# Two attention blocks on one core: the build order as a written list, some projections as column tiles, and eps sums on GpSimd

## The chip, the core and the metric

The kernel runs on one core of one Trainium2 chip. The metric is device microseconds per execution, from start to end of the program on that core. A run of the kernel is timed several times, and the median is given; a profile of one execution gives the span (first to last instruction) and what each engine did.

The engines: TensorE (PE in the profile, its weight loads PEld), VectorE (DVE), ScalarE (ACT), GpSimd (POOL), and SyncE (SP), which issues most DMAs.

## The reference

Two attention blocks over 2048 tokens, 640 features and 32 heads of 20 columns; their outputs are concatenated.

```
# block A, four segments of 512 tokens, s = 0..3, causal inside a segment
logits = q_s k_s^T * 20**-0.5 + mask
a_dot  = softmax(logits) v_s
a_mem  = (phi(q_s) M) / (phi(q_s) z + 1e-6)      # phi(t) = t+1 if t > 0 else exp(t)
o      = sigmoid(beta) * a_mem + (1 - sigmoid(beta)) * a_dot
M += phi(k_s)^T v_s;  z += sum(phi(k_s))
out_A = concat(o) wo_A
# block B, causal with a sliding window of 256 tokens
out_B = softmax(masked q k^T * 20**-0.5) v wo_B
```

Everything is bfloat16 outside, with float32 sums on the chip.

## The kernel before

The work is cut into eight chunks of 512 tokens, taken in turn: A0, B0, A1, B1, A2, B2, A3, B3. For each chunk PE makes q and k (`qk_job`, five pieces each, five matmuls of 512 columns a piece), v (`v_job`, two halves of four token tiles, five matmuls of 320 columns each), the scores (`score_batch`, L758), the products of weights and v (`av`, L827; `av_tile`, L848, in the last chunk), for A1 to A3 the product with the memory (`mem`), and the output projection (`final_job`, `last_job`). Projection and memory matmuls go through one helper, `wide` (L870), which issues a single 128x128 matmul.

Three shapes of matmul tile follow each other on PE: scores use four row groups of 20 rows (four heads at once; some batches, on the edge squares of the masks, have key tiles of 64 columns: 64 small matmuls in a batch); `av` uses four column tiles of 32 columns at tile positions (0, 32j), again four heads at once; `wide` and `dm_job`, which updates the memory, use the whole array.

PSUM holds three double banks for scores (`sc`) and two single banks (`m`, made by `bank()`) for everything else. A group of `wide` matmuls or an `av` fills one of the two; it is free again when VectorE has copied it (L501, L677, L682, L1027) or transposed it into `tt` (`turn`, L883).

ScalarE turns each score bank into exps (`pt`, L774). GpSimd cuts the masks out of them (`affine_select`, L813), VectorE does the masks of the edge batches by a product with `ends` (L791). After an `av` or a `mem`, `norm` works on the transposed tile: a reciprocal of the sums (L908), and on GpSimd the product with it (L918). For a `mem` the sums first get eps added on VectorE (L903), then the reciprocal (L906), the product goes to `u`, and VectorE adds `u` to `o` (L931).

The order of all this is set when the program is built. `Flow` keeps a clock for each engine with prices for each kind of work (`on_pe`, `on_dve`, `on_pool`, `on_act`, `on_dma`). The loop in `body` asks at each step what can run at the PE clock: first the next batch of scores (unless `may_wait()` says that ScalarE has enough), then the first of `pend` (`av` and `mem` in the order in which they came up, a `mem` right behind its `av`), then the first job of `jobs + fins` (projections as generators that yield what they wait for). `room()` holds score batches and `av` back when more than 160 PE matmuls were issued in the last 3000 ns of this clock. Work for VectorE, GpSimd and the DMA queue is issued by `at`, `when_idle` and `blocked` as the clocks pass. On the chip each engine then runs its instructions in that order and waits on semaphores.

## Time and profile before

| what | value |
|---|---|
| the three timed runs | 336.43, 333.79, 334.89 us, median 334.89 |
| the profiled execution | 334.4 us, its span 331.6 us |
| PE matmuls busy | 315.6 us, 6583 instructions (6619 weight loads, 174.4 us) |
| ScalarE | 302.4 us, 333 instructions |
| VectorE | 264.2 us, 556 instructions |
| GpSimd | 256.3 us, 648 instructions |
| exps (L774) | 306, 1012 ns mean |
| masks on GpSimd (L813) | 512, 374 ns mean |
| transposes (L883) | 88, 711 ns mean |
| eps sums on VectorE (L903) | 24, 371 ns mean |
| granted PE clock | 1.000 |

The table is of the profiled execution but for its first row. Busy times of one engine can overlap: a matmul's time runs until its result is out, and the next one starts earlier, so what one matmul costs is read from the distance of starts. The chain of work that ended last goes back from the last instruction to what released it, step by step. In a row of waits the numbers are the total in us, how many times, and the longest. In a timeline row they are the start, the time until the end of the last merged instruction, the engine, the line, and how many were merged.

### The profile page before, as it was taken

The numbers are of one execution on the slowest core, as the hardware profiler recorded it, in microseconds if no ns is written. First come the engines' busy times: TensorE is split into PE (matmuls) and PEld (weight loads), VectorE is DVE, ScalarE is ACT, GpSimd is POOL, SyncE is SP. The second block draws the span as 40 slices with busy tenths as digits, with TensorE's granted clock in tenths as the row PEclk, the third lists the DMA queues.
The fourth block names the chain that finished last, engine by engine and source line by source line (L and its number), as shares of the span: only waits on it lengthen the run. The fifth ranks groups of instructions, "written<-read, shape, count | busy, mean of one in ns | idle before, by whom it ended". The sixth has DMA issues, their size and how long they took to land.

```text
span 331.6 us, 15794 instructions
## 1 busy us (share of the span) xinstructions
PE 315.6 (95%) x6583; PEld 174.4 (53%) x6619; DVE 264.2 (80%) x556; ACT 302.4 (91%) x333; POOL 256.3 (77%) x648
## 2 busy tenths in 40 slices
PE   8999999999999999989999999999999999999896
PEld 3444546455444455546644545455654545666564
DVE  6777767798978899989868898888667889876654
ACT  1979999999999999999999999989999999999841
POOL 8366689998659799975867879996875969977750
DMA  6975746566596852335699145044555154769852
GB/s 198 396 253 152 173 135 125 136 175 176 132 226 132 165 155 63 67 86 122 183 208 181 42 94 156 3 104 80 148 140 114 21 150 122 166 142 187 178 127 100
DMA packets 76260, 47.36 MB, mean 143 GB/s; under 512 B 48381, under 2 KB 73181, under 8 KB 76189
## 3 DMA queue, kind: packets, MB, share of 16 engines
q1 hardware_dynamic: 75469, 45.71, 56.7%
q8 instruction: 51, 0.84, 1.1%
q10 hardware_dynamic: 720, 0.66, 0.7%
q14 instruction: 20, 0.16, 0.2%
HBM read 17.62 MB, written 16.96 MB: 104 GB/s over the span
## 4 chain that ended last, share of the span: by engine, by line
PE 57%; DVE 15%; ACT 10%; issue 7%; POOL 6%; DMA 3%; SPq 1%; ACTq 0%; DVEq 0%; POOLq 0%
PE m L870 36%; PE sc L758 11%; ACT pt L774 10%; PE m L827 6%; POOL pt L813 4%; DVE pt L791 4%; PE m L848 2%; DVE tt L883 2%; POOL u L918 2%; DVE pq L542 2%; DVE kA L501 2%; DVE vA L677 1%; DMA xT<-in_A_x_dram 1%; DVE pq L536 1%; DVE ot L1027 1%
## 5 line engine op out<-in xcount | busy, mean ns | idle before, releaser
L774 ACT ACTIVATE pt<-sc 128x1024 bf16<-128x1024 f32 (+2 forms) x306 | 285.0, 1012 | 10.7 <-PE sc L758 8.6
L813 POOL TENSOR_SCALAR_AFFINE_SELECT pt<-pt 128x128 bf16<-128x128 bf16 (+1 forms) x512 | 177.1, 374 | 60.4 <-ACT pt L774 57.4
L883 DVE STREAM_TRANSPOSE tt<-m 128x512 f32<-128x512 f32 x88 | 61.4, 711 | 20.0 <-PE m L827 9.1
L918 POOL TENSOR_TENSOR o<-tt,rr 128x320 bf16<-128x320 f32 x64 | 47.8, 747 | 4.1 <-DVE rr L908 4.0
L870 PEld LDWEIGHTS <-xT 128*128 128x128 bf16 x350 | 32.0, 97 | 24.2 <-issue 12.3
L758 PE MATMUL sc<-qB,kB 20*64 20x64 bf16 (+2 forms) x1728 | 38.6, 218 | 1.4 <-issue 0.8
L791 DVE TENSOR_TENSOR pt<-pt,ends 128x1024 bf16<-128x1024 bf16 (+2 forms) x50 | 36.3, 740 | 0.0
L758 PEld LDWEIGHTS <-kB 20*64 20x64 bf16 (+1 forms) x1728 | 21.7, 98 | 23.3 <-issue 22.0
L758 PE MATMUL sc<-qA,kA 20*64 20x64 bf16 (+4 forms) x1024 | 33.1, 237 | 0.5
L1027 DVE CAST ot<-m 128x320 bf16<-128x320 f32 x56 | 26.9, 485 | 7.4 <-PE m L870 7.1
L870 PEld LDWEIGHTS <-oT 128*128 128x128 bf16 x280 | 24.7, 98 | 11.4 <-issue 1.1
L870 PE MATMUL m<-wBv,xT 128*128 128x320 bf16 x160 | 27.0, 299 | 2.4 <-DVE tt L883 2.3
L870 PE MATMUL m<-wv_A,xT 128*128 128x320 bf16 x160 | 26.0, 299 | 2.0 <-DVE vA L677 1.9
L870 PE MATMUL m<-xT,wBq 128*128 128x512 bf16 x96 | 26.4, 381 | 0.4 <-issue 0.2
L870 PE MATMUL m<-xT,wq_A 128*128 128x512 bf16 x88 | 25.0, 381 | 1.8 <-DVE vA L677 0.8
L870 PE MATMUL m<-xT,wk_A 128*128 128x512 bf16 x96 | 25.6, 388 | 1.1 <-DVE qA L501 0.7
L870 PE MATMUL m<-xT,wBk 128*128 128x512 bf16 x84 | 24.8, 381 | 0.8
L758 PEld LDWEIGHTS <-kA 20*128 20x128 bf16 (+1 forms) x1024 | 13.5, 97 | 20.6 <-issue 19.6
L827 PE MATMUL m<-pt,vA 128*32 128x192 bf16 (+3 forms) x512 | 23.6, 275 | 0.0
L870 PE MATMUL m<-wo_A,oT 128*128 128x320 bf16 x140 | 22.7, 300 | 0.2
L501 DVE CAST kB<-m 128x512 bf16<-128x512 f32 x20 | 13.8, 691 | 9.4 <-PE m L870 9.4
L870 PE MATMUL m<-wo_B,oT 128*128 128x320 bf16 x120 | 19.4, 300 | 0.3 <-DVE ot L1027 0.3
(112 smaller groups left out, 405.3 us busy)
## 6 DMA issues: line engine op xcount, KB each, us to landing
out_dram<-ot SPq DMA_DIRECT2D x29, 160.0 KB
scr_o<-o SPq DMA_DIRECT2D x28, 160.0 KB
xT<-in_B_x_dram SPq DMA_DIRECT2D x8, 288.0 KB
xT<-in_A_x_dram SPq DMA_DIRECT2D x8, 256.0 KB
scr_pk<-e SPq DMA_DIRECT2D x15, 128.0 KB
vS<-vA SPq DMA_DIRECT2D x16, 87.0 KB
vL<-vB SPq DMA_DIRECT2D x8, 174.0 KB
scr_kA<-kA SPq DMA_DIRECT2D x16, 60.0 KB
```

What stands on the lines that cost most here:

```text
L501: nc.vector.tensor_copy(out=dst[:, m, at:at + L], in_=ps[:, :])
L542: nc.vector.tensor_tensor(out=r if len(box) == 1 else e, in0=r, in1=e, op=ALU.min)
L758: nc.tensor.matmul(ps[j // 2][h0:h1, j % 2, c0:c0 + nq], lhsT=k[rows, g, k0:k0 + h1 - h0], rhs=q[rows, g, q0:q0 + nq], start=True, stop=Tr ...
L774: nc.scalar.activation(out=pt[:, :, lo:hi], in_=ps[i][:, :, lo:hi], func=ACT.Exp, scale=self.scale)
L791: nc.vector.tensor_tensor(out=blk, in0=blk, in1=self.ends[:, c0, :].unsqueeze(1).unsqueeze(1) .to_broadcast([P, 2, n // SH, SH]), op=ALU.mult)
L813: nc.gpsimd.affine_select(out=blk, in_=blk, pattern=pat, compare_op=ALU.is_ge, fill=self.zero, base=base, channel_multiplier=mul)
L827: nc.tensor.matmul(O[HD * j:HD * j + HD, q0:q0 + nq], lhsT=v[:, at_head(h):at_head(h) + HD], rhs=pts[j // 2][:, j % 2, c0:c0 + nq], start= ...
L848: nc.tensor.matmul(O[HD * j:HD * j + HD, o0:o0 + nq], lhsT=v[:, at_head(h):at_head(h) + HD], rhs=pts[j // 2][:, j % 2, c0:c0 + nq], start= ...
L870: self.nc.tensor.matmul(ps[:, 0:n], lhsT=lhsT, rhs=rhs, start=start, stop=stop)
L883: self.nc.vector.transpose(out=tt[:], in_=O[:, :])
L918: nc.gpsimd.tensor_tensor(out=to[:] if add_to else to, in0=a, in1=b, op=ALU.mult)
L1027: nc.vector.tensor_copy(out=ot[:, 320 * hf:320 * hf + 320], in_=ps[:, 0:320])
```

## The change

A list, `PLAN`, now says what the builder's loop does next. Its marks: `S` or `s` is a batch of scores, `A` an `av` (or `av_tile`), `M` a `mem`; `q20*5` is five steps of the job that makes q of chunk 2 from piece 0 on, and k, v, o, d (the memory's update) and z (the last block) likewise. The loop takes only the item that the list wants and moves its PE clock on until the item can run; the old conditions hold only where the list has ended. `M` has a queue of its own (`memq`) and is no longer bound to come right behind its `A`; it needs the `norm` of that `A` to have been issued.

A capital `S` says more: if an `A` follows before the next batch of scores, all `wide` matmuls in between (projections and `mem`) are issued as four column tiles of 32 columns, the shape of the `A`.

The sum with eps for a `mem` is made by GpSimd (`s0`), ahead of the reciprocal on VectorE (`s1`). The other edits are to the builder's clock: a limit of one block of 256 PE instructions per 3900 ns in place of `room()`, new prices for some VectorE work, and a model of GpSimd and VectorE holding each other up (`held`).

```
+PLAN = (
+    "k00*5 q00*5 k01*4 S k01 q01*5 S v00*16 S v00*4 k02 S k02*4 k03*5 q02*3 S q02*2 q03*5 k04*5 "
+    "A S A q04*5 v01 s v01*9 s k10*5 S v01*10 S q10*2 A S q10*3 q11*3 S q11*2 q12*5 A s k11*5 "
...
+    "q14*2 A q14 S d2*5 v11*4 S v11*8 S v11*3 A v11 S v11*4 d2*2 S q20*4 A s q20*5 s q20*6 "
...
+    "k30*6 S k30*4 q30 S q30*4 A s M q30*5 v30*2 s v30*3 A S M v30*10 s A M s v30*5 q33*4 S q33 "
...
+    "S q40*2 d4*2 A s M k40*5 s q40*10 S v40*5 k40*5 A S k40*5 v40*5 S v40*2 A v40*2 S v40*6 "
...
+    "o60*5 o70*5 S o70*2 A S o70*3 o71*5 o60*4 S o60*10 s o60 A o60*5 o71*5 o60*3 A o60*7 o72*2 "
+    "z0*4 ")
...
     def on_pe(self, mode, ns, cols, ready=0.0, n=1):
-        self.issued.append((max(self.pe, ready), n))
-        return self.on_pe_(mode, ns, cols, ready)
+        self.count += 1
...
+        self.on_pe_(mode, ns, cols, ready)
+        first, self.sent = self.sent, self.sent + 2 * n
+        at = (first - BLOCK0) // BLOCK + 1
+        while BLOCK * at + BLOCK0 <= self.sent:
...
+            wait = self.block - x
+            if wait > 0.0:
...
+                self.pe += wait
...
+            self.block = x + BLOCK_NS
+            at += 1
+        return self.pe + 215.0
...
     def wide(self, ps, lhsT, rhs, n, start, stop):
 
-        self.nc.tensor.matmul(ps[:, 0:n], lhsT=lhsT, rhs=rhs, start=start, stop=stop)
-        self.f.on_pe("full", mm_ns(n), n)
+        f = self.f
+        if self.by_tiles:
+            for j in range(4):
+                s = slice(HD * j, HD * j + HD)
+                self.nc.tensor.matmul(ps[s, 0:n], lhsT=lhsT[:, s], rhs=rhs, start=start,
+                                      stop=stop, tile_position=(0, HD * j),
+                                      skip_group_check=True)
+            f.on_pe("col", n / 2.4 + COL_NS, n, 0.0, 4)
+        else:
+            self.nc.tensor.matmul(ps[:, 0:n], lhsT=lhsT, rhs=rhs, start=start, stop=stop,
+                                  skip_group_check=True)
+            f.on_pe("full", mm_ns(n), n)
...
-        def s1():
+        def s0():
+            nc.gpsimd.tensor_single_scalar(out=rr[:], in_=tv[:, :, DH], scalar=EPS, op=ALU.add)
+            t = f.on_pool(EPS_NS, t0)
+            f.when_idle(t, lambda: s1(t))
+
+        def s1(te=None):
             if add_to:
-                nc.vector.tensor_single_scalar(out=rr[:], in_=tv[:, :, DH], scalar=EPS,
-                                               op=ALU.add)
-                f.on_dve(100.0, t0)
                 nc.vector.reciprocal(out=rr[:], in_=rr[:])
+                t1 = f.on_dve(276.0, te)
...
-        f.when_idle(t0, s1)
+        if add_to:
+            f.at(t0 - 100.0, s0)
+        else:
+            f.when_idle(t0, s1)
...
+        plan = PLAN.split()
+        plan = [x.split("*")[0] for x in plan for _ in range(int((x + "*1").split("*")[1]))]
+        visits, tiles = [False], False
+        for x in plan:
+            if x in "Ss":
+                visits.append(False)
+                tiles = x == "S"
+            elif x == "A" and tiles:
+                visits[-1] = True
...
+            want = plan[-1] if plan else None
+            self.by_tiles = bool(plan) and visits[i]
+            if i < len(bs) and want in (None, "S", "s"):
...
-                        if t <= f.pe and not self.may_wait():
+                        if t <= f.pe and (want or not self.may_wait()):
+                            if want:
+                                plan.pop()
...
-                                    pend.append((n, g, "mem"))
+                                    memq.append((n, g))
...
-            if pend:
+            if pend and want in (None, "A"):
...
+            if memq and want in (None, "M"):
+                n, g = memq[0]
...
+                if want and jb[2] != want and (jb[2][0] != "d" or jb[1] in ("bank", 0.0)):
+                    continue
```

## The prediction, made before the changed kernel ran

> **What bounds the kernel now.** I read the page's busy row first, then the chain of work that ended last, the timeline of short stretches, the waits of PE, and the DMA queues.

> ```profile
> span 331.6 us, 15794 instructions
> PE 315.6 (95%) x6583; PEld 174.4 (53%) x6619; DVE 264.2 (80%) x556; ACT 302.4 (91%) x333; POOL 256.3 (77%) x648
> ...
> PE 57%; DVE 15%; ACT 10%; issue 7%; POOL 6%; DMA 3%; SPq 1%; ACTq 0%; DVEq 0%; POOLq 0%
> ```

> PE is busy nearly throughout and owns 57% of the chain; ACT follows closely. ACT has more room than 91% says: in the timeline 12 exps of 1024 elements from 96.47 take 11.51 us, 0.96 each, though one lasts 1.03, so durations overlap. Hence PE. The timeline shows what PE's busy time hides:

> ```profile
> 103.70 0.40 PE L758 MATMUL sc<-qA,kA 20*128 20x320 bf16 x8
> 104.03 0.31 PE L870 MATMUL m<-wBv,xT 128*128 128x320 bf16 x1
> 104.27 0.59 PE L827 MATMUL m<-pt,vA 128*32 128x448 bf16 x12
> 104.60 0.25 PEld L827 LDWEIGHTS <-vS 128*32 128x32 bf16 x16
> 104.68 0.29 PE L827 MATMUL m<-pt,vS 128*32 128x64 bf16 x16
> 104.94 0.39 PE L870 MATMUL m<-pq,MZ 128*128 128x512 bf16 x1
> 105.26 0.42 PE L758 MATMUL sc<-qA,kA 20*128 20x448 bf16 x8
> ```

> Five 512-column matmuls at 17.04 are followed by other work at 18.11: 0.214 each, 2.4 columns per ns. So the 320 columns at 104.03 need 0.133, yet the next kind of tile starts 0.24 later; the 512 columns at 104.94 need 0.213, the next starts 0.32 later. Each change between tile shapes (scores 20 rows, full 128x128, columns 128x32) thus costs about 0.10. I put all PE matmuls of the trace in order of time: 383 runs of one shape, 382 changes, with medians of 91 to 99 ns beyond streaming (115 after the 64-column scores). 382 x 0.097 = 37 us of the span.

> The gaps that are left come to some 18 us after the first 6 us of loading; where two weight loads but one matmul are recorded a record is missing, and I left those out. Most wait for DVE to empty one of the two PSUM banks:

> ```profile
> PE m L870 <- DVE vA L677: 2.7, 4, 0.8
> PE m L870 <- DVE tt L883: 2.3, 12, 0.2
> ...
> PEld L827 <- DVE rr L906: 2.0, 6, 0.4
> ```

> One gap has no semaphore at all, inside a run of scores:

> ```profile
> 312.95 0.23 PE L758 MATMUL sc<-qB,kB 20*128 20x128 bf16 x3
> 314.02 0.39 PE L758 MATMUL sc<-qB,kB 20*128 20x128 bf16 x13 [0.84 <-issue]
> ```

> ```profile
> q8 instruction: 51, 0.84, 1.1%
> ```

> 0.84 MB over 6583 + 6619 PE instructions is 64 B each, so these 51 packets carry PE's program, 256 instructions at a time. The gap follows the densest stretch: 256 PE instructions within 2.06 us from 309.3. I read it as program that came late.

> **The change, part by part.** The sum is made against the profiled execution: 334.4 us, span 331.6 and 2.8 around it; the median of the three runs, 334.9, lies 0.5 above it.

> *Fewer changes of shape.* I expanded PLAN: 153 score batches (102 S, 51 s), 64 A, 24 M. In 54 visits an A follows a capital S, and there every projection matmul and M is cut into four column tiles, the shape of the A itself. Counted in order, the list has 322 changes (two of them at the very end, in the last block's transposes, as before), 60 fewer. 60 x 0.097 = -5.8 us; bounds -5.5 (0.091) and -6.9 (0.115). It counts in full, since PE carries the chain.

> *The tiles.* 220 projection matmuls and 9 M become four each. In the rows above 12 column matmuls (three quads, 448 + 320 + 192 = 960 columns, 0.400 us of streaming) start at 104.27 and the next at 104.68: 0.41. The four run side by side, so I take 0; a few ns each would be +0.7. Hiding them is the streaming of the quad before; without that cover, see the third rival.

> *More program.* 229 x 3 x 2 = 1374 more PE instructions, 10%, five more packets: nothing on average (one packet in 6 us). Locally it counts: a tiled A of a B chunk (104 instructions, 0.70 us) directly before the batch of 64-column scores (128 in 0.68) with some tiled projections (8 in 0.136) puts 256 instructions in under 2.5 us. Laid out by such spacings, the list has 12 spots of this kind; the trace of before has three, one with the 0.84 stall (1.0 against the matmul's normal start). At one in three, four stalls: +4.0 less the one there now, +3.0. Bounds: -1.0 (none), +11.0 (all 12).

> *The order, and M apart from A.* Before, an A is followed at once by its M, both banks then hold work for DVE's transposes (0.72 each), and the same waits recur in each of the three memory chunks (102.38, 181.07 and 258.17: 0.39 each; 115.75, 194.44, 271.54: 0.34), with smaller ones 1.4 us a chunk, 4.2 in all. In the list 12 of 24 M come in a later visit than their A: -2.1. Larger single waits for DVE (84.81: 0.9; 142.07: 0.9; 153.30: 0.7; 231.89: 0.8; 76.4, 132.5 and 211.3: 0.3 to 0.5) sum to 4.6; I let under half go, -1.9. Together -4.0. Bounds: -11 (all but the unavoidable rest) and +8: the list is strict, so an A whose mask is late now holds PE where the old loop took other work, and 64 A at 0.12 are 8. Nearest is the gain, as PE waits 18 us today and not zero. Behind a waiting A stand all later PE work and, through it, ACT. Where DVE's wait goes, ACT's exps are late next: ACT waits 8.6 us for scores today.

> *Sums of eps to GpSimd.* 24 DVE instructions go (371 ns mean, 8.9 us); 24 come on GpSimd. Its nearest rows: 203 ns for 4 elements (ez at L342), 413 for 36 (MZ at L651), 727 for 320. So 24 x 0.2 to 0.7, +5 to +17 us of busy; I take 0.25, as 16 elements lie nearest the first: +6. Cover: GpSimd stands idle 57.4 us waiting for exps, so on the path 0. Cover gone: the masks queued behind come late, and A's with them; bounds -0.8 (DVE freed on the chain) and +7. The added wait is GpSimd's for the transpose; behind it stand masks and norms.

> *DMAs and edits of the clock.* No DMA is added or removed; q/k regroup stores and loads (4 + 4 each), v copies, pk and pq stores, output stores and transposes move with their jobs on SP, which is in order. SP itself waits for data (23.0 us for o at L949 alone), so I take 0; if kA's round trip (4.2 us on the chain from 81 to 88.8) were late once more, +4. New prices of the builder's clock run nothing on the chip.

> Sum: -5.8 + 0 + 3.0 - 4.0 + 0 + 0 = -6.8; 334.4 - 6.8 = 327.6 us.

> **The rivals.**

> 1. *Program fetch takes it all (slower).* Place: tiled A's before 64-column scores. For: the stall at 314.02. Against: two of three dense spots passed. All 12 stall: -5.8 - 1.0 + 11.0 = +4.2, 338.6 us, if the waits for DVE shrink by only 1. It decides from about 10 stalls of 1.0 us (they must eat 5.8 + 4.0). Chance 0.15.

> 2. *PE is no longer the pace.* ACT, or GpSimd with the eps, holds what PE saves:

> ```profile
> 120.00:140.00 20.00, 19.25 (x446) 10.96 (x451) 18.97 (x40) 19.46 (x22) 20.00 (x43) 1.00 0.34 91
> ...
> 200.00:220.00 20.00, 18.90 (x445) 11.00 (x441) 17.77 (x37) 18.85 (x22) 20.00 (x41) 1.00 0.35 88
> ```

> GpSimd (fifth pair) is full in these two stretches, and eps sums fall in them. Against: an exp waited for a mask only 0.6 us in all. If each of the 24 delays the path by 0.25, +6.0 on top of -6.8: 333.6. The eps row itself hints at blocking: on DVE it took 153 to 1010 ns, median 255, for the same 16 elements. [...] Also in this case: the list is followed, but its order fits the chip no better than the old one. Chance 0.20, within 1%.

> 3. *Weight loads of the tiles are exposed.* 16 loads in 0.25 us are 16 ns each; 229 x 4 x 16 = 14.7: 334.4 - 6.8 + 14.7 = 342.3. Against: the 0.41 for 960 columns. [...] Chance 0.03.

> **How the numbers follow.** Forecast 0.62: 319.5 to 331.5, the low end with waits cut by 11 and fetch +2 (-5.8 - 11 + 2 = -14.8). One per cent, 3.3 us, is about what a measurement of this kernel can tell from no change. Faster by over 1% (below 331.5): 0.62. Within 1%: the second rival, 0.20. Slower: 0.15 + 0.03 = 0.18. The range for 8 in 10 goes from 319.5 to 338, just short of the first rival's value.

> **What would show it.** Right: PE matmuls at L827's shape on projection tiles, about 322 changes of shape, quads of 320 columns 0.136 apart, four or fewer gaps of about 1 us with "issue" as releaser and no semaphore, about 56 program packets, DVE busy down by 9, waits of PE for DVE down by a quarter. Wrong: many such gaps behind tiled A's; PE waiting for masks (L813); GpSimd at 20 of 20 in more stretches; exps closer to 0.90 apart everywhere, which would mean that ACT sets the time.

## The result, and the profile after

The changed kernel took 336.2 us (median of 22 runs, 332.81 to 339.06), the kernel before 334.26 (22 runs, 332.8 to 336.43) beside it. The ratio is 1.0049, interval 1.0027 to 1.0071: half a per cent slower, where 327.6 us was forecast. (Ratios leave out runs far above a kernel's fastest, so a ratio can lie below the quotient of two medians.) The profiled execution took 334.67 us, span 333.0. Its page, in the rows that were shown of before:

```profile
span 333.0 us, 17212 instructions
...
PE 316.1 (95%) x7315; PEld 177.5 (53%) x7315; DVE 255.2 (77%) x533; ACT 299.7 (90%) x333; POOL 266.7 (80%) x672
...
q8 instruction: 57, 0.93, 1.1%
...
PE 47%; DVE 8%; ACT 6%; POOL 4%; DMA 4%; issue 4%; SPq 1%; ACTq 0%; DVEq 0%; POOLq 0%
```

The chain of this profile could be followed back only to 83 us, so its shares sum to about 75%; PE's 47% is 63% of what the chain covers, and can't be set beside the 57% of before as it stands.

What the diff should do is all there: about 700 more matmuls and as many more weight loads, six more program packets, DVE down by 9.0 us, GpSimd up by 10.4. Put in order of time, PE's matmuls make 323 runs of one shape (383 before), 322 changes as forecast. The timeline of PE shows the tiles (start, time to the end of the last merged instruction, what):

```profile
311.83 0.40 PE L814 MATMUL sc<-qB,kB 20*128 20x128 bf16 x16
312.16 0.46 PE L930 MATMUL m<-wo_B,xT 128*32 128x320 bf16 x8
312.48 0.30 PE L904 MATMUL m<-pt,vB 128*32 128x128 bf16 x8
```

Eight column matmuls, two quads of 320 columns, need 0.27 us of streaming at 2.4 columns per ns (five matmuls of 512 columns took 1.07 us from 17.04 in the profile of before), and the `av` after them starts 0.32 after their start; one after the other the eight would need 1.07. Before, one full matmul of 320 columns held the next kind up for 0.24, of which 0.13 is streaming. The tiles do run side by side, and of the 0.11 for the change of shape 0.05 is left here; the median of 41 such places in this trace is 0.02.

PE still did not finish sooner. I added up PE's time beyond streaming, missing records put back: 76.5 us before, 77.3 after. Changes of shape fell by 5.8; gaps without a semaphore rose by 2.0 (1.25 to 3.25); waits on other engines and on DMAs rose by 4.2 (17.1 to 21.3). The totals are the firm part; how they divide depends on the price that a change is given. (PE's idle time alone, where a semaphore or a DMA ended it, rose from 8.6 to 9.8 us.) PE's waits for VectorE's copies of v, most of the larger ones that the prediction named, fell from 3.1 to 0.9 us, but others have come. The timeline near 80 us, then near 316:

```profile
79.24 0.49 DVE L733 TENSOR_TENSOR vA<-m,omg 128x320 bf16<-128x320 f32 x1 [0.96 <-DMA vS<-vA]
...
79.78 0.29 PE L883 MATMUL m<-pt,vX 128*32 128x256 bf16 x4 [0.50 <-DVE vA L733]
```

```profile
316.51 0.85 PE L935 MATMUL m<-wo_B,xT 128*128 128x320 bf16 x5 [1.85 <-DMA xT<-scr_o]
...
318.36 1.94 ACT L830 ACTIVATE pt<-sc 128x1024 bf16<-128x1024 f32 x2 [2.20 <-PE sc L814]
```

At 79.78 the list wants an `A`, and both banks are full: VectorE copies v out of one only when an older DMA, which still reads the buffer, is done; it stood 0.96 us for that before 79.24, and PE 0.50. (A wait of 0.47 for VectorE follows at 81.63, and one of 0.82 for a mask product of VectorE stands at 296.13.) At 316.51 it wants `o71`, whose transposed rows have not landed. Items behind it that could have run are not tried, and 1.85 us of idle PE become 2.20 us in which ScalarE waits for scores. ScalarE's waits for scores, before and after (total, times, longest):

```profile
ACT pt L774 <- PE sc L758: 8.6, 20, 1.5
```

```profile
ACT pt L830 <- PE sc L814: 14.6, 26, 2.2
```

Where the time lies is read from the first exp of each chunk. Before: 9.1, 48.0, 88.6, 123.1, 167.2, 201.7, 244.3, 278.8 us, last exp 317.2. After: 9.3, 48.1, 89.0, 123.0, 168.1, 202.3, 245.3, 279.2, last exp 321.1. Up to 279 us the two kernels run level, although PE is ahead in work: at the last chunk's first scores 170 matmuls of the output projection are left (a quad of column tiles counted as one), before 210. The last chunk takes 41.9 us in place of 38.4; the end behind it is shorter (31 of these matmuls left after the last score where there were 60, 13.3 us from the last batch of scores to the end where it was 15.8).

### The profile page after: what moved, and what is told of

It is laid out like the page before. It is cut to its first block, busy times and chain, and to the rows that moved or that the text cites. A ratio compares the mean times of both kernels' runs of the same rounds, so it can differ in the third digit from the quotient of the medians.

```text
span 333.0 us, 17212 instructions
## 1 busy us (share of the span) xinstructions
PE 316.1 (95%) x7315; PEld 177.5 (53%) x7315; DVE 255.2 (77%) x533; ACT 299.7 (90%) x333; POOL 266.7 (80%) x672
## 4 chain that ended last, share of the span: by engine, by line
PE 47%; DVE 8%; ACT 6%; POOL 4%; DMA 4%; issue 4%; SPq 1%; ACTq 0%; DVEq 0%; POOLq 0%
PE m L935 23%; PE sc L814 9%; PE m L930 7%; PE m L883 6%; ACT pt L830 5%; DVE tt L949 4%; POOL pt L869 2%; PE m L904 1%; DMA scr_pk<-e 1%; DMA xT<-scr_o 1%; DMA scr_o<-o 1%; DMA vS<-vA 1%; POOL o L987 1%; PE m L686 1%; POOL u L987 1%
## 5 line engine op out<-in xcount | busy, mean ns | idle before, releaser
L830 ACT ACTIVATE pt<-sc 128x1024 bf16<-128x1024 f32 (+2 forms) x306 | 283.0, 1026 | 16.7 <-PE sc L814 14.6
L949 DVE STREAM_TRANSPOSE tt<-m 128x512 f32<-128x512 f32 x88 | 61.0, 708 | 24.3 <-PE m L883 14.5
L935 PEld LDWEIGHTS <-xT 128*128 128x128 bf16 x289 | 26.4, 97 | 19.3 <-issue 6.1
L935 PEld LDWEIGHTS <-oT 128*128 128x128 bf16 x229 | 20.3, 97 | 12.9 <-issue 3.9
L814 PEld LDWEIGHTS <-kA 20*128 20x128 bf16 (+1 forms) x1024 | 13.3, 97 | 22.1 <-issue 21.1
L935 PE MATMUL m<-wBv,xT 128*128 128x320 bf16 x142 | 23.1, 299 | 1.1 <-DVE tt L949 0.4
L883 PE MATMUL m<-pt,vA 128*32 128x192 bf16 (+3 forms) x512 | 23.5, 274 | 0.4
L935 PE MATMUL m<-wo_A,oT 128*128 128x320 bf16 x116 | 19.8, 300 | 1.7 <-DVE kA L557 0.8
L935 PE MATMUL m<-wv_A,xT 128*128 128x320 bf16 x119 | 19.8, 300 | 0.4 <-issue 0.2
L935 PE MATMUL m<-xT,wBq 128*128 128x512 bf16 x77 | 19.6, 380 | 0.3 <-DVE tt L949 0.3
L935 PE MATMUL m<-xT,wBk 128*128 128x512 bf16 x74 | 19.2, 380 | 0.0
L557 DVE CAST qB<-m 128x512 bf16<-128x512 f32 x20 | 13.8, 688 | 7.0 <-PE m L930 4.3
L935 PE MATMUL m<-xT,wk_A 128*128 128x512 bf16 x69 | 18.3, 387 | 0.7 <-DMA xT<-in_A_x_dram 0.6
L738 DVE CAST vB<-m 128x320 bf16<-128x320 f32 x32 | 15.5, 484 | 4.2 <-PE m L930 2.7
```

Source lines behind the costliest of these rows:

```text
L557: nc.vector.tensor_copy(out=dst[:, m, at:at + L], in_=ps[:, :])
L738: nc.vector.tensor_copy(out=dst, in_=src)
L814: nc.tensor.matmul(ps[j // 2][h0:h1, j % 2, c0:c0 + nq], lhsT=k[rows, g, k0:k0 + h1 - h0], rhs=q[rows, g, q0:q0 + nq], start=True, stop=Tr ...
L830: nc.scalar.activation(out=pt[:, :, lo:hi], in_=ps[i][:, :, lo:hi], func=ACT.Exp, scale=self.scale)
L883: nc.tensor.matmul(O[HD * j:HD * j + HD, q0:q0 + nq], lhsT=v[:, at_head(h):at_head(h) + HD], rhs=pts[j // 2][:, j % 2, c0:c0 + nq], start= ...
L935: self.nc.tensor.matmul(ps[:, 0:n], lhsT=lhsT, rhs=rhs, start=start, stop=stop, skip_group_check=True)
```

## The experiments

The sixteen runs below come in four groups of four, each group on one chip together with the kernel before (334.55, 333.88, 334.25 and 334.08 us); ratios are to that one. The theory after the two traces: what PE saves is lost again where the strict list meets a late item or late program, above all in the last chunk. The rivals: the tiles themselves or the eps sums cost the time, or PE was never the pace and ScalarE is. Each run lists its mean granted PE clock, and that became a third question. I call a run at full clock when this mean is at least 0.998.

**The change again, without tiles, and with eps on VectorE.**

a_again is the changed kernel without an edit.

> The changed kernel once more, unaltered, for a second profile and the granted clock of each run. Theory A (ScalarE's exps set the pace, so PE's savings are swallowed, and late score banks cost what they last): about 336 us, with spans that grow as the mean granted clock falls from 1.000 to 0.99 (335 at 1.000, 337.5 at 0.99). Theory B (PE is the pace and the tiles cost as much as the changes of shape save): the same time, with no relation to the clock.

Measured: 337.34 us (12 runs), ratio 1.0089 (1.0059 to 1.012). The granted clock is below 0.998 in 9 of the 12 runs (median 337.96) and at least 0.998 in three (335.1 to 336.8, median 335.3), while all 35 runs of the kernel before have 0.999 or more. So part of the loss is a lower clock, part is not.

```
-            self.by_tiles = bool(plan) and visits[i]
+            self.by_tiles = False
```

> The list is kept, but all projections stay full 128x128 matmuls: some 60 changes of tile shape come back (5.8 us of PE) and 1392 PE instructions go. Theory A: little moves, 334 to 337.5 us; the gaps of PE without a semaphore (about 3 us in all after the change) fall below 1 us and make up for part of the changes of shape. Theory B, tiles have a hidden cost: at least 4 us faster than the changed kernel (below 332). Theory B', PE sets the pace and the tiles are a clean gain: about 6 us slower (342).

Measured: 339.09 us, ratio 1.005 (1.002 to 1.0081); 10 of 12 runs at the lower clock (339.9), two at the full one (334.8). The spread, 7 us, hides the worth of the tiles; they were measured again below, on a steadier list.

```
-        def s0():
-            nc.gpsimd.tensor_single_scalar(out=rr[:], in_=tv[:, :, DH], scalar=EPS, op=ALU.add)
...
             if add_to:
+                nc.vector.tensor_single_scalar(out=rr[:], in_=tv[:, :, DH], scalar=EPS,
+                                               op=ALU.add)
                 nc.vector.reciprocal(out=rr[:], in_=rr[:])
```

> Only the eps sums go back to VectorE (24 instructions, 8.9 us of VectorE before), the list and the tiles stay. Theory A: within 1.5 us of the changed kernel. Rival C (the sums on GpSimd delay masks and products): at least 3 us faster than the changed kernel (below 333.5).

Measured: 335.21 us, ratio 1.0033 (1.0009 to 1.0057), 2.1 us under a_again. That lies between the two expectations. Between runs at full clock the difference is 0.5 us (334.83 against 335.3). The edit also changes the builder's prices for this work, and by the traces the order of VectorE and of GpSimd moves in some places besides the sums, so the runs show what the edit is worth as a whole. In the changed kernel the sums are short, and VectorE waits for them seldom (source line: min, median, max in ns; then who waited, in us and times):

```profile
L968 POOL TENSOR_SCALAR rr<-tt x24: 263/265/591, 99.3 to 286.4; 128x16 f32<-128x16 f32 x24
...
  DVE rr L974: 2.0, 6
```

**The last chunk by the old rule.** The list is cut ahead of the last chunk's first batch (the 134th), and from there the old loop decides, with its old limit of 160 matmuls per 3000 ns and with full matmuls (`room()` and its calls are left out here):

```
...
+        k = [x for x, p in enumerate(plan) if p in "Ss"][133]
+        plan = plan[:k]
         plan.reverse()
...
```

> The list ends where the last chunk's scores begin; from there the old rule with its limit of 160 matmuls in 3 us orders the work, with full matmuls. Theory A: the last chunk, from its first to its last exp, goes from 41.9 us back to 38 to 39.5, and the kernel takes 332 to 334 us. Theory B (a loss spread over all stages): within 1 us of the changed kernel.

Measured: 334.38 us, ratio 0.999 (0.9967 to 1.0014); the last chunk takes 39.4 us from first to last exp where it took 41.9. Against a_again it is about 3 us less, 2.3 between runs at full clock. The edit takes away the strict list and the tiles of that chunk together, and a_lastfull below, which takes away the tiles alone, comes to nearly the same ratio (1.0, on another chip): how much of this the strict list costs is not shown. The rest is not gained, and 8 of 12 runs had a lower clock (334.72 against 332.96). Stretches of this execution show why (PE, PEld, DVE, ACT, POOL busy with counts, granted clock, DMA share, GB/s):

```profile
78.21:81.62 3.41, 1.77 (x88) 1.00 (x88) 1.33 (x4) 2.92 (x4) 1.46 (x4) 1.00 0.59 123
81.62:85.03 3.41, 2.77 (x71) 1.73 (x62) 3.19 (x8) 2.33 (x3) 3.02 (x8) 0.50 0.28 81
85.03:88.44 3.41, 3.37 (x34) 1.71 (x32) 3.16 (x8) 2.21 (x4) 1.09 (x3) 1.00 0.66 125
```

The wait near 80 us leaves PE busy for 1.77 us, about half of a stretch of 3.41 us, and the next 3.41 us run at a granted clock of 0.50.

**Is PE the pace, or ScalarE?** Two kernels on the old order. b_peless leaves out one matmul of five in each of the 56 output-projection groups, 7.5 us of PE (`wide` issues nothing while `skip` is set):

```
...
+                        self.skip = m == 2
                         self.wide(ps, lhs(m), wo[:, hf, m, :], 320,
                                   m == 0, m == self.KT - 1)
+                        self.skip = False
```

> The kernel before, in its own order, but each of the 56 output-projection groups that go through the two single banks leaves out one of its five matmuls: 56 x 0.133 = 7.5 us of PE work less, and a wrong output. Theory A (ScalarE sets the pace through most of the kernel, and PE work that is saved there turns into waiting): 1 to 4 us faster. Theory P (PE sets the pace, as the prediction had it): 6 to 7.5 us faster.

Measured: 333.13 us, ratio 0.9977 (0.9948 to 1.0006). The four runs at full clock have a median of 331.5 (three from 331.1 to 331.6, one at 334.6), 2.3 under the kernel before; 6 runs had a lower clock (333.5).

b_actless leaves out 36 of the 1024 columns of the larger exps from the second chunk on, 252 exps, 7.5 us of ScalarE (the smallest distance of two such exps falls from 903 to 873 ns):

```
+            cut = 18 if hi - lo == 512 and n >= 19 else 0
-            nc.scalar.activation(out=pt[:, :, lo:hi], in_=ps[i][:, :, lo:hi], func=ACT.Exp,
+            nc.scalar.activation(out=pt[:, :, lo:hi - cut], in_=ps[i][:, :, lo:hi - cut],
...
```

> The kernel before, in its own order, but from the second chunk on each exp of 1024 columns does 988 and leaves the rest of the tile as it was: some 245 exps x 30 ns = 7.4 us of ScalarE work less, and a wrong output. Theory A: 4 to 7 us faster. Theory P: less than 2 us faster.

Measured: 333.13 us, ratio 0.9977 (0.9958 to 0.9996), all runs at full clock. ScalarE's time beyond its best spacing rose from 23.0 to 29.7 us: what it saved it waited. Both theories fall. 7.5 us off PE bring 2.3 at full clock (0.75 by the medians), 7.5 off ScalarE bring 0.75: neither alone is the pace. Each runs in a fixed order and each waits for the other. By the traces both keep the order of the kernel before.

**Two late items of the list.** a_lastfull takes the tiles away in the last chunk alone, which thins PE's program there:

```
-            self.by_tiles = bool(plan) and visits[i]
+            self.by_tiles = bool(plan) and visits[i] and i < 134
```

> The changed kernel with its list, but in the last chunk the projections stay full matmuls, so that PE's program is thinner there by about 400 instructions, at the price of 14 changes of tile shape more (1.4 us). Theory A (late program costs 1.7 us in the last chunk): the gaps without a semaphore between 296 and 312 us shrink from 1.7 to under 0.7 us; the time stays within 1.5 us of the changed kernel, since the 2.0 us wait for the transposed output rows stays. If late program were the main loss: 2 us or more faster.

Measured: 335.48 us, ratio 1.0 (0.997 to 1.003). In the last chunk of this execution one clear gap without a semaphore is left, 0.59 us beyond streaming, where the changed kernel's profile has three (0.42, 0.59 and 0.68); that is as expected. But such gaps differ from execution to execution: a_v21_o71_full below, without tiles there too, has two of 2.1 and 0.9, so thinner program alone does not end them. The three runs at full clock have a median of 332.3. PE waits 3.09 us for the transposed rows, and the clock drops to 0.50 behind that. Stretches of this execution, in the same columns:

```profile
313.22:316.63 3.41, 1.08 (x8) 0.80 (x9) 0.19 (x1) 0.76 (x1) 0.27 (x1) 1.00 0.85 132
316.63:320.04 3.41, 3.41 (x29) 1.66 (x26) 2.48 (x5) 1.94 (x2) 1.17 (x3) 0.50 0.19 60
320.04:323.45 3.41, 3.22 (x94) 2.16 (x93) 1.76 (x4) 1.94 (x2) 2.00 (x6) 1.00 0.38 103
```

The late rows are the larger wait in this chunk. a_v21late moves the v piece that waits near 80 us behind k and the output projection (the part of the list that changes, two of its lines joined):

```
- A s v21*5 k23*3 S k23*2 A s o00*5 k23*5 v21*5 S
+ A s k23*5 k23*3 S k23*2 A s o00*5 v21*10 S
```

> The changed kernel, in its list one step moved: the first group of v of chunk 2's second half comes eleven steps later, so that its copy on VectorE no longer waits for the store of the first half. Theory of the clock (a stretch in which PE streams little is followed by 3.41 us at half clock): PE's wait at 79.8 us goes, hardly any run keeps a mean clock of 0.995 or lower, and the median comes to about 334.7, the time of the changed kernel's runs at full clock. Without that theory: median and clocks as for the changed kernel (336 to 337, three runs in four below 0.998).

Measured: 335.59 us, ratio 0.9995 (0.9961 to 1.0029). The wait at 79.8 is gone and the third chunk starts at 87.5, where the profiles with the old place of v have 88.4 to 90.6. But PE waits 2.30 us for the transposed rows before 315.97, ScalarE 3.18 for scores behind it, and the clock drops to 0.50 at 316.8, behind a stretch with PE busy for 1.12 us. What was expected of the clock missed: 7 of 12 runs have 0.995 or less (335.99 in the median), the five at full clock 333.4. a_o71late moves `o71` behind other projections (again the part that changes):

```
- S o70*3 o71*5 o60*4 S o60*10 s o60 A o60*5 o71*5 o60*3 A o60*7 o72*2
+ S o70*3 o60*4 S o60*10 s o60 A o60*5 o71*5 o60*3 A o60*2 o71*5 o60*5 o72*2
```

> The changed kernel, in its list one step moved at the end: the first half of the output projection o71 comes after the last scores, so that PE no longer stands at 316.5 us until the transposed rows have landed. Theory S (the strict list stops PE at items that are late, and the gaps draw half clock behind them): the wait of 2.0 us at 316.5 and the stage at half clock behind it go; 333 to 334.5 us, 2 us less than the changed kernel. Rival (the list is as good as its model and the loss is tiles and program): no change beyond 1 us.

Measured: 336.86 us, ratio 1.0073 (1.0045 to 1.01): missed. The wait at 316.5 is gone and the last chunk takes 39.6, but the wait near 80 us is still there, with half clock from 82.2 to 85.6 in this execution. The clock is not all of it: the five runs at full clock have 336.6. Both moves together, and both with the last chunk untiled:

> Both moved steps together: v of chunk 2's second half later, o71 later. Theory S: the last chunk starts at 277 us (278.8 before) and takes 39 to 40 us; most runs at full clock; 330.5 to 332.5 us, which is faster than the kernel before by 0.5 to 1.2%. Rival: 335 to 336, as with either alone.

Measured: 334.53 us, ratio 1.0006 (0.998 to 1.0032), 10 of 12 runs at full clock: missed, the 2 to 4 us did not come. In its profile six gaps without a semaphore, of 0.59 to 1.25 us beyond streaming, sum to 5.6 us.

> Both moved steps, and full matmuls in the last chunk. Theory S with late program as a part of it: the gaps without a semaphore in the last chunk (1.7 us) go, 14 changes of shape (1.4 us) come back: within 1 us of the kernel with both steps moved. If late program weighs more than its gaps: more than 1 us faster than that.

Measured: 333.46 us, ratio 0.9967 (0.9939 to 0.9995). A third of a per cent faster than before; the interval overlaps that of a_v21_o71, so the two are not told apart.

**The old last chunk and the later v.** a_old_v21 has the edits of a_oldlast and a_v21late:

> The list up to the last chunk, with v of chunk 2's second half later, and the old rule with its limit in the last chunk. Theory S: no half clock at 81 us any more (mean clock at 0.998 or more in most runs), last chunk near 38.5 us: 330.5 to 332 us. Rival (the clock falls whatever the order, because PE streams less in all): clocks of 0.995 in half of the runs or more, 333 to 335 us.

Measured: 331.58 us (6 runs), ratio 0.9923 (0.9898 to 0.9949): the fastest list up to here. Its profile has a gap of 2.04 us without a semaphore, which ends at 304.86 and leaves PE busy for 1.37 us of its stretch; the next stretch runs at half clock. So such a gap was followed by the drop as well.

**What stayed open: the clock, the tiles, the eps sums.** b_stall is the kernel before with one PSUM copy, at 137 us, made six times, so that PE finds no free bank:

```
+                for _ in range(6 if (n, what, m) == (4, "k", 2) else 1):
                     nc.vector.tensor_copy(out=dst[:, m, at:at + L], in_=ps[:, :])
```

> The kernel before with one stall put in: at 137 us one copy of a PSUM bank on VectorE is made six times over instead of once (3.4 us of VectorE more, the same values), so that PE stands for 2 to 3 us. Theory of the clock: behind it come 3.41 us at half clock in most runs (mean clock 0.995, which no run of the kernel before shows), and the kernel is 4 to 5 us slower. Rival (the clock falls for another reason): all runs at 0.999 or 1.000, and 2 to 3.4 us slower.

Measured: 337.75 us (4 runs), ratio 1.0101 (1.0065 to 1.0138), all four runs at a clock of 0.995 or less. Timeline of PE, then stretches, of this kernel:

```profile
138.62 0.71 PE L759 MATMUL sc<-qB,kB 20*64 20x64 bf16 x64
142.91 3.52 PE L871 MATMUL m<-wv_A,xT 128*128 128x320 bf16 x14 [3.58 <-DVE kA L502]
```

```profile
139.91:143.32 3.41, 0.41 (x4) 0.30 (x4) 3.27 (x6) 2.06 (x3) 1.58 (x5) 1.00 0.69 141
143.32:146.73 3.41, 3.41 (x25) 1.77 (x22) 2.81 (x8) 0.00 (x0) 0.73 (x1) 0.50 0.03 5
146.73:150.14 3.41, 3.41 (x83) 1.78 (x71) 3.00 (x7) 3.10 (x4) 1.90 (x5) 1.00 0.25 73
```

A wait made on purpose, 3.58 us in this execution, brings the half clock (0.50 from 143.32 to 146.73), in a kernel whose runs never fell below 0.998. This one is shown by an intervention, not read off a coincidence. Wait and half clock together cost 3.7 us, where 4 to 5 were expected.

c_best repeats a_old_v21; the next takes its tiles away (as in a_notiles); the last brings its eps sums back to VectorE (as in a_epsdve).

> Repeats the list up to the last chunk, v of chunk 2's second half later, old rule in the last chunk: 331 to 332.5 us, a ratio of 0.990 to 0.996 to the kernel before.

Measured: 331.94 us (12 runs), ratio 0.9931 (0.9904 to 0.9959); 7 runs at full clock have 330.78, 5 at 0.995 have 333.26.

> The same without column tiles: 46 changes of shape come back (4.5 us of PE), over 1000 PE instructions go. If PE work counts by a third, as where output projections were thinned: 1 to 2.5 us slower than c_best. If the tiles are worth nothing: within 1 us.

Measured: 333.61 us, ratio 0.9996 (0.9977 to 1.0016), all at full clock. Changes of shape go from 327 to 391, and the time by 1.7 us, 2.8 between runs at full clock. The intervals do not touch: the edit costs time, so the tiles help. (With the tiles the builder's prices change too, and some of VectorE's and GpSimd's order with them.)

> The same as c_best with the eps sums on VectorE: within 1 us of c_best; if GpSimd's queue is hurt by the sums, 1 us or more faster.

Measured: 329.78 us (6 runs), ratio 0.9872 (0.9846 to 0.9897), all at 0.998 or more. It beats both kernels, and c_best by 2.2 us (1.0 against c_best's runs at full clock); as in a_epsdve, some of the order moves with the edit. ScalarE waits for scores 10.1 us, between before (8.6) and after (14.6):

```profile
span 327.4 us, 17125 instructions
...
PE 314.8 (96%) x7264; PEld 177.4 (54%) x7264; DVE 260.9 (80%) x559; ACT 298.5 (91%) x332; POOL 256.9 (78%) x648
```

```profile
ACT pt L844 <- PE sc L828: 10.1, 21, 1.9
```

## Why the prediction was wrong

The measured 336.2 us lies inside the stated range (319.5 to 338), which was wide; the gain of 6.8 us is what failed to come. In PE's own sum the terms forecast were -5.8, +3.0 and -4.0; those measured are -5.8, +2.0 and +4.2. So the term that failed is the order, and what failed with it is the step that counted PE's saved time in full.

*Fewer changes of shape, -5.8, "It counts in full, since PE carries the chain".* The count was right: 322 changes, and 5.8 us less of PE's time. What failed is the conversion into time. The first profile said PE 95% busy and 57% of the chain; b_peless then shows that 7.5 us of PE are worth 2.3 us at full clock (0.31 each), and the tiles of c_best, 64 changes or 6.2 us at 0.097, are worth 1.7 to 2.8. The prediction looked at ScalarE (91%) and decided between the two; b_peless and b_actless show that neither is the pace. The rows to read were the 8.6 us that ScalarE waits for PE and the 17 us that PE waits for others: each engine already spent time on the other. For the second rival that was the right place ("its order fits the chip no better than the old one", and eps). Its case, within 1% of before, is the one that came. Its 333.6 us lies 1.1 under the profiled execution but 2.6 under the median; the first rival's 338.6 lies 2.4 above the median, so by the number alone neither is clearly nearer, and the first one's 11 us of gaps were not there.

*The tiles, 0.* Right: hardly a cost per tile shows. The third rival is gone: two quads took 0.32 us, 0.05 beyond their streaming, where eight exposed loads at 16 ns would have added 0.13.

*More program, +3.0.* About right in this execution: gaps without a semaphore rose from 1.25 to 3.25 us; a_again's has three of 0.6, 1.5 and 2.2 us. That execution has no wait near 316, and its last chunk takes 42.1 us all the same. In the profiles of before and after, such gaps of 0.19 us and more ended 1.3 to 1.6 us after one of the program packets had landed; that the program came late is a reading of these distances, and no run shows it apart. One inside a run of 64-column scores, in the timeline of the changed kernel (a packet had landed at 302.42):

```profile
302.97 0.48 PE L814 MATMUL sc<-qB,kB 20*64 20x64 bf16 x37
303.86 0.31 PE L814 MATMUL sc<-qB,kB 20*64 20x64 bf16 x27 [0.41 <-issue]
```

In no profile did they come near the 11 us of the first rival.

*The order, -4.0.* Wrong in sign: PE's waits rose by 4.2, within the stated bounds (-11 to +8). A part of the old waits went as forecast (those for copies of v from 3.1 to 0.9 us), and new ones took their place. The upper bound's reason, "the list is strict", is what the traces show, at two places that the runs name: the last chunk (about 3 us, a_oldlast under a_again, list and tiles together) and the v piece near 80 us (0.999 in a_oldlast, 0.9923 and 0.9931 without it: 2.0 to 2.2 us, clock included). With both mended the ratio goes from 1.0089 (a_again) to 0.9931 (c_best), about 5 us. The rest of the list is not bad: c_best_eps is 4.3 us under the kernel before, 1.7 of it by the tiles.

*Sums of eps, 0.* Mis-sized: 0.5 to 2.2 us, though DVE fell by 9 us and only 2.0 us of waits for the sums show. The 6 us of GpSimd taken for them was about right (6.7), and the sums themselves were hardly held up: 23 of 24 took 263 to 275 ns. Most likely idle time of GpSimd elsewhere was not cover at the places where the sums fall, but which later work they delay was not traced, and the order that moves with the edit is a rival left open.

*DMAs, 0.* No DMA was added, but the waits near 80 and near 316 end with one, a v copy and the transposed rows. The prediction named SP's order and the round trip of kA; it did not ask of each item of the list whether its data would be there.

*Not in the prediction at all: the clock.* The profile of before says 1.000 throughout, so no term had it. Of the changed kernel's first 22 runs, 15 have less than 0.998 (335.9 to 339.1); the seven at 0.998 or more have a median of 334.67, level with before. One stretch of 3.41 us at half clock lowers the mean by about 0.005, so 0.995 stands for one and 0.990 for two. Runs with a lower clock are longer by 1.8 us in a_oldlast and by 2.5 in c_best. One stretch at half clock loses at most half of itself, 1.7 us (from 317.59 in a_lastfull, at half clock, ten matmuls of 320 columns are followed by the next work after 2.65 us; from 307.47 in the profile of before, at full clock, after 1.47), so a part of this is the longer waits that bring the drop. So in sum: at full clock the changed kernel's gains and new waits cancel, and longer waits with the half clock behind them make it slower.

What stays open: how the loss in the last chunk divides between the strict list, the tiles and the gaps without a semaphore; whether these gaps are late program, and why they last 0.6 us in one execution and 2 in another; which wait each saved microsecond of PE became; and a list without such gaps, which was not tried.

## What to carry to other kernels

A high busy share and a high share of the chain do not make an engine's time count in full: where two engines at 90% wait for each other in fixed orders, expect a part of what one saves (about a third here), and measure it by leaving a known amount out. A strict order needs one question for each item, whether its data can have landed on a disturbed run, because a late item stops all behind it (PE for 1.85 us at 316.51 here). Count a wait of PE that leaves it busy for 1.77 us or less of a stretch of 3.41 at more than its length, since half clock can follow: it did in eight executions here, and runs with a lower clock were longer by 1.8 us in a_oldlast and 2.5 in c_best.

## What the runs showed of the hardware

*Gaps without a semaphore on PE, and what landed before them.* The program packets (57 after, 51 before) have 16 KB each, and 0.93 MB over 7315 matmuls and 7315 weight loads is 64 B an instruction, so 256 to a packet. PE stood without a semaphore for 0.84 us before 314.02 in the profile of before, and for 0.19 to 0.52 us before 73.12, 206.63, 300.14, 303.86 and 308.96 in that of the changed kernel. A packet had landed 1.52 us ahead of the first of these ends, and 1.40, 1.31, 1.31, 1.44 and 1.61 ahead of the others. The gaps named above in other runs go up to 2.2 us (a_again), at other places. That they are program that comes late is the author's reading.
